# Attention and FFN on one core: the last 1024 queries in five chunks in place of three, and another rank for finishing attention

## The chip, the cores and the metric
The kernel runs on one core of a Trainium2 chip. The metric is device time in microseconds of one execution; the number shown for a kernel is the median of its runs. The core has five engines that run side by side: TensorE (PE: matmuls, with weight loads shown as PEld), VectorE (DVE), ScalarE (ACT), GpSimd (POOL) and SyncE (SP, which here issues DMAs). They wait for one another by semaphores. Matmuls write to PSUM, eight banks of 128 x 512 fp32; the rest lives in SBUF.

## The reference
One pre-layernorm transformer block in bfloat16: sequence S = 2048, width D = 512, 32 heads of 16, FFN width F = 1792.

```python
h  = x + attention(layernorm(x))        # softmax(q k^T / 4) v per head, then @ wo
h2 = h + (gelu(ln(h) @ w_gate) * (ln(h) @ w_up)) @ w_down
```

## The kernel before
**Work.** Scores are made transposed: a *tile* is 128 keys x 512 score columns of one head group, so that exp of it is at once the stationary-side partner of V. Queries come in chunks, `CHUNKS = (512, 512, 512, 256, 256)` (line 1143). A *unit* is one PSUM bank of attention output: 64 tiles (16 key blocks x 4 row groups g). In a chunk of 512 a unit is one head slot; in a chunk of 256 it holds two slots side by side (`per(c) = 512 // CHUNKS[c]`, line 1290). There are 32 units and 2048 tiles for any choice of chunks. One tile's scores are one matmul (line 1532, 32 rows of the array, row group g); its product with V is one matmul per slot (lines 1694 to 1697, a 32-column group of the array each, four groups at once).

**Exp on two engines.** ScalarE takes two tiles per instruction (line 1585) from PSUM banks 0 to 3. VectorE takes tiles in groups of four from the other banks (`dget`, line 1599): one conversion per tile (line 1658), then a chain of three operations for the group (lines 1671, 1673, 1678) with a quarter of the middle one on GpSimd (line 1675). A tile made so needs two products with V per slot, as its value is the product of two fp16 factors accumulated in PSUM.

**End of a unit** (`ofin`, line 1758): VectorE copies the bank to `OA` (line 1762), SP issues a transpose by DMA (line 1769; PE turns the last unit, line 1774), VectorE takes the reciprocal of the softmax sums (line 1778), GpSimd (VectorE for the last unit) multiplies into `Otok` (line 1784). When all units of a chunk have ended, `Otok` is turned (line 1807), and per block of 128 queries `post` (line 1825) projects with `wo`, adds the residual (1845), makes the layernorm (1849 to 1854) and turns the result into `hnT_c` (1857; the last chunk uses PE, 1835 and 1862).

**FFN of a chunk**, beside the attention of the chunks that follow: gates into PSUM (line 1883, through the helper at line 1324), copied to `GUT` (1912); one Gelu over the chunk in two halves on ScalarE (1925), with a table load ahead of it and one back to exp after it; ups, multiplied in place by VectorE (1939); downs per block of 128 queries (1949), the residual add (1958) and the store (1961). The last chunk, behind the last exp, takes Gelu straight from PSUM (1908). `GUT` has 512 query columns; every chunk starts at column 0, and the gates of a chunk wait until the downs of all earlier ones are done (line 1890). A bank is packed with 512 // CHUNKS[c] blocks of F (line 1870).

**Order.** Nothing is ordered by hand: `Sched` (line 889) simulates the engines at build time with a cost per operation and emits, for each engine, the ready operation of lowest rank; ties are spread by a seeded random number (line 906). The chip then runs each engine's list in that order. Ranks that matter here: VectorE's conversions and FFN evacuations stand at -2.2 (`HELD`, line 1117, used in `_rank`, line 934), the chain of a VectorE group at -2.1 or -4 (line 1574), and `ofin` at -3 until its copy is out and at -1 after it (line 1708). FFN matmuls are raised to -6 while `room()` holds, that is while few exp tiles wait for their product with V (`HLAG`, lines 1118 and 2013). `behind()` (line 1310) lets VectorE hold one tile less in PSUM when the FFN of finished chunks lags. `fill` (line 1991) puts matmuls with a zero operand where PE would idle, until 15 of the 16 query blocks are through their downs. A second, safe path (`max_path`) stands in the program and is entered only if a check of the softmax sums at the end asks for it; it does not run here.

**Space.** `h_c` and `hnT_c` of a chunk lie in the part of `QT` that the chunk's end has freed, or in the block of chunk 0 or 1 (`h_at`, line 1244).

Of the kernel before, what the change touches and what calls it, by code (L numbers as in the profile page):

```python
# [888 lines left out]
class Sched:  # L889
# [5 lines left out]
    def __init__(self, P, banks):  # L895
        self.P = P
        self.t = {n: 0.0 for n in P.ENGINES}
        self.done = {}
        self.streams = []
        self.banks = [(0.0, b) for b in banks]  # L900
        self.now = 0.0
        self.fill = None
        self.debt = (0.0, 0.0)
        self.pipe = 0.0
        self.lent = set()
        self.rng = random.Random(16)
# [298 lines left out]
def fast_path(nc, P, base0, ARENA, pbank, flag, A_x, A_wqkv, A_wo, B_x, B_w_gate, B_w_up, B_w_down, out):  # L1205
# [38 lines left out]
    def h_at(c):  # L1244

        if 128 * first_t[c + 1] % 512 == 0:
            c4 = 128 * first_t[c + 1] // 512 - 1
            return 8192 * c4, [("qT", s_, c4) for s_ in range(NSLOT)]
# [7 lines left out]
    h_over = [k for _, k in h_off]  # L1256
# [51 lines left out]
    PIECES = sum(2 * NFC // (512 // n) + n // 128 for n in CHUNKS[:-1])  # L1308

    def behind():  # L1310
        rest = (len(TILES) - C["qpos"]) / (len(TILES) * (1 - CHUNKS[0] / 2048))
# [211 lines left out]
    def scores(put):  # L1523
        fns, rd = [], []
        for i, b in put:
            u, kt, g = TILES[i]
            c, slots = units[u]
            c4, qs = qpart(c)
            n, j = len(slots), slots[0] // 2
            rhs = QT[32 * g:32 * g + 32, c4, slots[0], qs] if n == 1 else QT[32 * g:32 * g + 32, c4, slots[0]:slots[0] + n, qs]  # L1530
            o = pbank[:, b, :] if n == 1 else pbank[:, b, :].rearrange("p (s q) -> p s q", s=n)
            fns.append(MM(o, KT[32 * g:32 * g + 32, j, 128 * kt:128 * kt + 128], rhs, True, True, (32 * g, 0)))
            rd += [("qT", x, c4) for x in slots] + [("kT", j, kt // 4)]
        return fns, sorted(set(rd))

    def qk():
        nxt, an = 0, 0
# [25 lines left out]
    def qk_ready(u):  # L1563
        c, slots = units[u]
        c4, _ = qpart(c)
        keys = [("qT", x, c4) for x in slots] + [("kT", slots[0] // 2, q) for q in range(NCH)]
        return all(k in P.last_writer and sch.done[P.last_writer[k]] <= sch.now for k in keys)

    def close_group():
# [188 lines left out]
    def ofin(u):  # L1758
# [66 lines left out]
    def post(c, qt):  # L1825
# [4 lines left out]
        if c < NC - 1:  # L1830
            yield Wait(lambda: C["ot"] >= first_t[c] + qt + 1)
        else:
            b = yield Acquire(reads=rd, gate=lambda: C["oproj"] >= first_t[c])
            pt = pbank[:, b, :].bitcast(BF16)
            yield Op("pe", 4 * TTR, cols=512, fns=[lambda e, hc=hc: e.transpose(out=pt[:, 128 * hc:128 * hc + 128], in_=Otok[:, cp, qt, 128 * hc:128 * hc + 128], identity=ident[:])
                                 for hc in range(4)], reads=rd, writes=[("pb", b)])
# [37 lines left out]
    gbase = [0]  # L1874
    for c_ in range(NC):
        gbase.append(gbase[-1] + NFC // pack(c_))

    def product(c, k, b, w, rd):
        nq = CHUNKS[c]
        for j in range(pack(c)):  # L1880
            fc = k * pack(c) + j
            for hf in range(2):
                yield Op("pe", 2 * tmm(nq), cols=2 * nq, fns=[MM(pbank[:, b, j * nq:j * nq + nq], w[:, dc, 128 * fc:128 * fc + 128], hnT_c[c][:, :, dc, :], dc == 0, dc == 3)
                                                              for dc in (2 * hf, 2 * hf + 1)], reads=rd, writes=[("pb", b)])

    def gates(c):
        nb = CHUNKS[c] // 128
        rd = ["wg"] + [("hnT", c, q) for q in range(nb)]
        for k in range(NFC // pack(c)):
            b = yield Acquire(reads=rd, gate=lambda: C.get(("hnT", c), 0) == nb and C["down"] >= first_t[c])  # L1890
            yield from product(c, k, b, wg_sb, rd)
            sch.add(gate_evac(c, k, b), base_dl(c) + 29)

    def tmm(n):
        return max(0.09, TMM * n / 512)

    def dE():
        return P.retire([("x", 0, 0), ("x", 0, 1)] + [("x", c) for c in range(1, NCH)] + [("xn", i) for i in range(8)])

    def gslots(c, k):  # L1900
        n = pack(c)
        return GUT[:, n * k:n * k + n, 0:CHUNKS[c]], [("GUT", n * k + j) for j in range(n)]

    def gate_evac(c, k, b):
        o_ap, keys = gslots(c, k)
        i_ap = pbank[:, b, :].rearrange("p (f q) -> p f q", f=pack(c))
        if c == NC - 1:
            yield Op("act", 0.47, lambda e: e.activation(out=o_ap, in_=i_ap, func=ACT.Gelu_apprx_tanh), reads=[("pb", b)], writes=keys)
            sch.release(b)
            C[("gelu", c, k)] = 1  # L1910
            return
        yield Op("dve", 0.6, lambda e: e.tensor_copy(out=o_ap, in_=i_ap), reads=[("pb", b)], writes=keys, extra=dE)  # L1912
        sch.release(b)
        C[("gate", c)] = C.get(("gate", c), 0) + 1
        C["pieces"] += 1
        if C[("gate", c)] == NFC // pack(c):
            sch.add(gelu(c), -5)

    def gelu(c):
        nq = CHUNKS[c]  # L1920
        for hf in range(GSPLIT):
            f0, f1 = NFC * hf // GSPLIT, NFC * (hf + 1) // GSPLIT
            ap = GUT[:, f0:f1, 0:nq]
            keys = [("GUT", f) for f in range(f0, f1)]
            yield Op("act", 0.05 + 0.000833 * nq * (f1 - f0) + TTAB * (hf == 0) + TTAB * (hf == GSPLIT - 1), lambda e, ap=ap: e.activation(out=ap, in_=ap, func=ACT.Gelu_apprx_tanh), reads=keys, writes=keys)
            for k in range(f0 // pack(c), f1 // pack(c)):
                C[("gelu", c, k)] = 1

    def ups(c):
        rd = ["wu"] + [("hnT", c, q) for q in range(CHUNKS[c] // 128)]  # L1930
        for k in range(NFC // pack(c)):
            b = yield Acquire(reads=rd, gate=lambda: ("gelu", c, k) in C)
            yield from product(c, k, b, wu_sb, rd)
            sch.add(up_evac(c, k, b), base_dl(c) + 29)

    def up_evac(c, k, b):
        o_ap, keys = gslots(c, k)
        u_ap = pbank[:, b, :].rearrange("p (f q) -> p f q", f=pack(c))
        yield Op("dve", 0.6, lambda e: e.tensor_tensor(out=o_ap, in0=u_ap, in1=o_ap, op=ALU.mult), reads=[("pb", b)] + keys, writes=keys)  # L1939
        sch.release(b)  # L1940
        C["gut"] += 1
        C["pieces"] += 1

    def downs(c):
        for qt in range(CHUNKS[c] // 128):
            b = yield Acquire(reads=["wd"], gate=lambda: C["gut"] >= gbase[c + 1])
            for f0 in range(0, NFC, 3):
                fcs = list(range(f0, min(NFC, f0 + 3)))
                yield Op("pe", TMM * len(fcs), cols=512 * len(fcs), fns=[MM(pbank[:, b, :], GUT[:, fc, 128 * qt:128 * qt + 128], wd_sb[:, fc, :], fc == 0, fc == NFC - 1)
                                                                         for fc in fcs], reads=["wd"] + [("GUT", fc) for fc in fcs], writes=[("pb", b)])  # L1950
            C["down"] += 1
            C["pieces"] += 1
            sch.add(down_evac(c, qt, b), base_dl(c) + 29)

# [118 lines left out]
```

## Time and profile before
| | |
|---|---|
| median of 9 runs | 820.14 us (819.09 to 820.67) |
| the profiled execution: its own time, its span | 820.55 us, 818.5 us |
| busy over the span: ACT, PE, DVE, POOL | 93%, 94%, 91%, 30% |
| exps on ScalarE / on VectorE | 778 x 2 tiles / 492 tiles |
| fill matmuls (line 1989) | 120 |
| Gelus of chunks 0, 1, 2, 3 begin | 348.3, 526.7, 676.6, 779.6 us |
| last exp ends | 778.3 us |
| last output add begins | 812.9 us |

All times in the profile are from one execution. Times of a group are the sum of its instructions' durations; instructions of an engine overlap a little (an exp shows 1.09 us, and the next starts about 0.92 us after it), so that the distance from start to start is the price of one. TensorE's granted clock is 1.00 nearly throughout (0.90 after 800 us).

### The profile page before, as it was taken

How to read it: one execution, taken by the hardware profiler on the slowest of the kernel's cores; microseconds unless marked ns; L12 is line 12 of the kernel's file. 1: busy time of each engine (PE TensorE's matmuls, PEld its weight loads, DVE VectorE, ACT ScalarE, POOL GpSimd, SP SyncE). 2: the span in 40 equal slices, each digit the busy share in tenths (PEclk: the TensorE clock that was granted, in tenths of full speed). 3: DMA queues.
4: the chain of work that ended last, by engine and by line, in shares of the span. 5: the costliest groups of instructions: out<-in, count | busy, mean ns of one | idle time of the engine just before them, and what ended most of it. 6: DMA issues, size and time to landing. Idle time of an engine off the chain costs nothing. (4 is left out here: it accounts for less than half of the span.)

```text
span 818.5 us, 16590 instructions
## 1 busy us (share of the span) xinstructions
PE 772.4 (94%) x6438; PEld 239.7 (29%) x6500; DVE 744.7 (91%) x1217; ACT 764.1 (93%) x813; POOL 244.5 (30%) x292
## 2 busy tenths in 40 slices
PE   9899999989899999999989899999999998999997
PEld 4222222222222222232222222222233332333464
DVE  7669999899999999999999899999999998998762
ACT  2899999999999999999999999999999999999931
POOL 5703445632332532112222421212223221132200
PEclk9999999999999999999999999999999999999999
DMA  6200000620000210000000210000021000021000
GB/s 206 52 8 2 7 8 7 245 52 8 7 1 1 60 33 1 8 20 14 22 8 1 58 27 8 7 8 20 20 66 21 20 8 8 2 40 40 8 14 18
DMA packets 48776, 23.84 MB, mean 29 GB/s; under 512 B 38192, under 2 KB 47664, under 8 KB 48688
## 3 DMA queue, kind: packets, MB, share of 16 engines
q1 hardware_dynamic: 48688, 22.69, 10.3%
q8 instruction: 53, 0.87, 0.5%
q14 instruction: 35, 0.29, 0.1%
HBM read 11.80 MB, written 2.10 MB: 17 GB/s over the span
## 5 line engine op out<-in xcount | busy, mean ns | idle before, releaser
L1331 ACT ACTIVATE PT<-pbank 128x1024 bf16<-128x1024 f32 x778 | 722.9, 1092 | 13.4 <-PE pbank L1325 11.0
L1325 PE MATMUL pbank<-QT,KT 32*128 32x512 bf16 x2048 | 346.2, 384 | 24.4 <-ACT PT L1331 18.6
L1658 DVE TENSOR_SCALAR dXE<-pbank 128x512 uint16<-128x512 f32 x492 | 323.4, 685 | 11.2 <-PE pbank L1325 9.8
L1675 POOL TENSOR_TENSOR dXE<-dXE 128x512 f16<-128x512 f16 x123 | 154.2, 1253 | 455.2 <-DVE dXE L1673 455.2
L1325 PEld LDWEIGHTS pbank<-QT,KT 32*128 32x128 bf16 x2048 | 86.3, 91 | 326.3 <-ACT PT L1331 245.7
L1325 PE MATMUL pbank<-PT,VA 128*32 128x512 bf16 (+1 forms) x1948 | 129.0, 342 | 1.2 <-DVE h_c L1845 0.7
L1673 DVE TENSOR_TENSOR dXE<-dXE 128x1536 f16<-128x1536 f16 x123 | 118.0, 959 | 1.0
L1678 DVE TENSOR_SCALAR dXE<-dXE 128x2048 uint16<-128x2048 uint16 x123 | 86.5, 704 | 8.7 <-POOL dXE L1675 7.7
L1671 DVE TENSOR_SCALAR dXE<-dXE 128x2048 uint16<-128x2048 uint16 x123 | 89.0, 723 | 0.2
L1325 PE MATMUL pbank<-dXE,VA 128*32 128x512 f16 (+1 forms) x1224 | 75.7, 342 | 3.2 <-DVE dXE L1678 3.0
L1324 PE MATMUL pbank<-hnT_c,wg_sb 128*128 128x512 bf16 (+1 forms) x280 | 67.2, 340 | 0.0
L1324 PE MATMUL pbank<-hnT_c,wu_sb 128*128 128x512 bf16 (+1 forms) x280 | 60.3, 346 | 2.5 <-DVE GUT L1939 2.2
L1324 PE MATMUL pbank<-wd_sb,GUT 128*128 128x512 bf16 x205 | 55.1, 381 | 2.7 <-issue 2.5
L1325 PEld LDWEIGHTS pbank<-PT,VA 128*32 128x32 bf16 x1948 | 36.1, 95 | 62.8 <-issue 59.7
L1939 DVE TENSOR_TENSOR GUT<-pbank,GUT 128x512 bf16<-128x512 f32 x56 | 37.3, 683 | 10.6 <-PE pbank L1324 9.8
L1989 PE MATMUL pbank<-ones_bf,zero_bf 128*128 128x512 bf16 x120 | 42.7, 387 | 1.3 <-issue 1.3
L1324 PE MATMUL pbank<-xnT,wqkv_sb 128*128 128x512 bf16 x128 | 37.3, 383 | 0.8 <-DMA xnT<-xn_sb 0.8
L1912 DVE CAST GUT<-pbank 128x512 bf16<-128x512 f32 x49 | 33.4, 684 | 4.0 <-PE pbank L1324 4.0
L1478 POOL TENSOR_SCALAR QT<-QT,qmask 128x512 bf16<-128x512 bf16 x30 | 25.4, 851 | 24.7 <-DVE QT L1475 23.7
L1325 PEld LDWEIGHTS pbank<-dXE,VA 128*32 128x32 bf16 x1224 | 22.1, 95 | 33.5 <-issue 15.7
L1324 PEld LDWEIGHTS pbank<-hnT_c,wu_sb 128*128 128x128 bf16 x280 | 23.8, 99 | 26.2 <-issue 11.9
L1784 POOL TENSOR_TENSOR Otok<-OAT,LINV 128x256 bf16<-128x256 bf16 (+1 forms) x38 | 24.0, 639 | 12.8 <-DVE LINV L1778 11.9
(87 smaller groups left out, 334.4 us busy)
## 6 DMA issues: line engine op xcount, KB each, us to landing
xres<-in_A_x_dram SPq DMA_DIRECT2D x16, 128.0 KB, 2.1
out_dram<-out_sb SPq DMA_DIRECT2D x16, 128.0 KB, 1.7
wg_sb<-in_B_w_gate_dram SPq DMA_DIRECT2D x1, 1792.0 KB, 7.7
wu_sb<-in_B_w_up_dram SPq DMA_DIRECT2D x1, 1792.0 KB, 11.6
wd_sb<-in_B_w_down_dram SPq DMA_DIRECT2D x1, 1792.0 KB, 15.9
x_sb<-in_A_x_dram SPq DMA_DIRECT2D x3, 512.0 KB, 7.9
wqkv_sb<-in_A_wqkv_dram SPq DMA_DIRECT2D x1, 896.0 KB, 7.1
x_sb<-in_A_x_dram SPq DMA_DIRECT2D x2, 256.0 KB, 2.9
```

The source lines that it names most:

```text
L1324: return lambda e: e.matmul(o, l, r, start=start, stop=stop)
L1325: return lambda e: e.matmul(o, l, r, start=start, stop=stop, tile_position=tile)
L1331: return lambda e: e.activation(out=o, in_=i, func=func, **kw)
L1478: yield Op("pool", 0.85, lambda e, par=par: e.tensor_scalar(out=QT[:, c, 2 * j + par, :], in0=raw, scalar1=qmask[:, par:par + 1], scalar2= ...
L1658: yield Op("dve", 0.603, lambda e: e.tensor_scalar(out=dXE[G["k"] % NX][:, 0, j, :], in0=pbank[:, b, :], scalar1=XMIN + 1024.0 * CENTER, s ...
L1671: yield Op("dve", 0.07 + 0.133 * n, lambda e: e.tensor_scalar(out=W, in0=X, scalar1=0x3ff, scalar2=0xb800, op0=ALU.bitwise_and, op1=ALU.bi ...
L1673: yield Op("dve", 0.066 + 0.267 * nd, lambda e: e.tensor_tensor(out=W[:, 0:nd, :].bitcast(F16), in0=W[:, 0:nd, :].bitcast(F16), in1=X[:, 0 ...
L1675: yield Op("pool", TPOOL, lambda e, j=j: e.tensor_tensor(out=W[:, j, :].bitcast(F16), in0=W[:, j, :].bitcast(F16), in1=X[:, j, :].bitcast( ...
L1678: yield Op("dve", 0.07 + 0.133 * (h1 - h0), lambda e, h0=h0, h1=h1: e.tensor_scalar(out=X[:, h0:h1, :], in0=X[:, h0:h1, :], scalar1=0x7c00 ...
L1912: yield Op("dve", 0.6, lambda e: e.tensor_copy(out=o_ap, in_=i_ap), reads=[("pb", b)], writes=keys, extra=dE)
L1939: yield Op("dve", 0.6, lambda e: e.tensor_tensor(out=o_ap, in0=u_ap, in1=o_ap, op=ALU.mult), reads=[("pb", b)] + keys, writes=keys)
L1989: return Op("pe", TMM, lambda e: e.matmul(pbank[:, b, :], zero_bf[:], ones_bf[:], start=False, stop=False, skip_group_check=True), reads=[ ...
```

## The change
The three last chunks of 512, 256 and 256 queries become 256, 256, 256, 128 and 128. Chunks are given column ranges in `GUT`, so that chunks smaller than 512 can lie side by side and a chunk's gates wait only for chunks whose columns it takes. A unit of a 128-chunk holds four slots of 128 queries: scores of a tile take two matmuls of 256 columns (slots 0-1 and 2-3 have different keys), its products with V four of 128. The end of a unit ranks at -2.3 after its copy, in place of -1. `HLAG` is 6 in place of 8, and the seed is another.

```diff
-        self.rng = random.Random(16)
+        self.rng = random.Random(21)
...
-HLAG = 8
+HLAG = 6
...
-CHUNKS = (512, 512, 512, 256, 256)
+CHUNKS = (512, 512, 256, 256, 256, 128, 128)
...
-        c0 = h_spare.pop(0)
-        return 8192 * c0, [(k, c0, q) for k in ("h", "hnT") for q in range(4)]
+        if h_spare:
+            c0 = h_spare.pop(0)
+            return 8192 * c0, [(k, c0, q) for k in ("h", "hnT") for q in range(4)], first_t[c0 + 1]
+        c4 = 128 * first_t[c] // 512 - 1
+        assert CHUNKS[c] == 128 and CHUNKS[c - 2] == 256
+        return 8192 * c4 + 2048, [("qT", s_, c4) for s_ in range(NSLOT)], 0
...
-            fns.append(MM(o, KT[32 * g:32 * g + 32, j, 128 * kt:128 * kt + 128], rhs, True, True, (32 * g, 0)))
+            for jj in range(max(1, n // 2)):
+                oo, rr = (o, rhs) if n < 4 else (o[:, 2 * jj:2 * jj + 2, :], rhs[:, 2 * jj:2 * jj + 2, :])
+                fns.append((jj, MM(oo, KT[32 * g:32 * g + 32, j + jj, 128 * kt:128 * kt + 128], rr, True, True, (32 * g, 0))))
...
-            sch.add(ofin(u), -1.0).dyn = lambda: -3 if C["oa"] <= u else -1.0
+            sch.add(ofin(u), -1.0).dyn = lambda: -3 if C["oa"] <= u else -2.3
...
-        if otok_n[c] == NSLOT // per(c) - 2:
+        if otok_n[c] == max(1, NSLOT // per(c) - 2):
             sch.add(xres_loads(c), 60)
...
             sch.release(b)
+        yield Wait(lambda: C["down"] >= h_off[c][2])
         b2 = yield Acquire(reads=[("OH", qt), "wo"])
...
-    def pack(c):
-        return 512 // CHUNKS[c]
+    def packs(c):
+        n = 512 // CHUNKS[c]
+        return [(f, min(n, NFC - f)) for f in range(0, NFC, n)]
...
+        o_ = g_at[-1] + CHUNKS[c_ - 1] if c_ else 0
+        g_at.append(o_ if o_ + CHUNKS[c_] <= 512 else 0)
...
+    def gut_free(c):
+        return all(C.get(("down", d), 0) == CHUNKS[d] // 128 for d in range(c) if g_at[d] < g_at[c] + CHUNKS[c] and g_at[c] < g_at[d] + CHUNKS[d])
...
-            b = yield Acquire(reads=rd, gate=lambda: C.get(("hnT", c), 0) == nb and C["down"] >= first_t[c])
+            b = yield Acquire(reads=rd, gate=lambda: C.get(("hnT", c), 0) == nb and gut_free(c))
...
-        return max(0.09, TMM * n / 512)
+        return max(0.056, TMM * n / 512)
...
-        for hf in range(GSPLIT):
-            f0, f1 = NFC * hf // GSPLIT, NFC * (hf + 1) // GSPLIT
-            ap = GUT[:, f0:f1, 0:nq]
+        parts = [(0, NFC // 2), (NFC // 2, NFC)] if nq > 128 else [(0, NFC)]
+        for i, (f0, f1) in enumerate(parts):
+            ap = GUT[:, f0:f1, g_at[c]:g_at[c] + nq]
...
-            b = yield Acquire(reads=["wd"], gate=lambda: C["gut"] >= gbase[c + 1])
+            b = yield Acquire(reads=["wd"], gate=lambda: C.get(("gut", c), 0) == len(packs(c)))
```
By the new rule the chunks' first columns in `GUT` are 0, 0, 0, 256, 0, 256 and 384. The planner's costs of an evacuation and of a Gelu now follow its width (0.07 + 0.001042 us per column on VectorE, 0.05 + 0.00083 on ScalarE), and a 128-column matmul is planned at 0.056 us.

More of the change, by code (lines that the diff above doesn't have):

```diff
@@ L1247, in h_at @@
             c4 = 128 * first_t[c + 1] // 512 - 1
-            return 8192 * c4, [("qT", s_, c4) for s_ in range(NSLOT)]
-        c0 = h_spare.pop(0)
-        return 8192 * c0, [(k, c0, q) for k in ("h", "hnT") for q in range(4)]
+            return 8192 * c4, [("qT", s_, c4) for s_ in range(NSLOT)], 0
+        if h_spare:
[4 more added lines that the diff above has]
+        return 8192 * c4 + 2048, [("qT", s_, c4) for s_ in range(NSLOT)], 0
     h_spare = [0, 1]
@@ L1255, in fast_path @@
     h_off = [h_at(c) for c in range(NC)]
-    h_over = [k for _, k in h_off]
+    h_over = [o[1] for o in h_off]
     h_c = [at("h_c%d" % c, [128, CHUNKS[c] // 128, D], BF16, h_off[c][0]) for c in range(NC)]
@@ L1307, in fast_path @@
     otok_n = {}
-    PIECES = sum(2 * NFC // (512 // n) + n // 128 for n in CHUNKS[:-1])
+    PIECES = sum(2 * -(-NFC // (512 // n)) + n // 128 for n in CHUNKS[:-1])
     def behind():
@@ L1531, in scores @@
             o = pbank[:, b, :] if n == 1 else pbank[:, b, :].rearrange("p (s q) -> p s q", s=n)
-            fns.append(MM(o, KT[32 * g:32 * g + 32, j, 128 * kt:128 * kt + 128], rhs, True, True, (32 * g, 0)))
-            rd += [("qT", x, c4) for x in slots] + [("kT", j, kt // 4)]
-        return fns, sorted(set(rd))
+            for jj in range(max(1, n // 2)):
+                oo, rr = (o, rhs) if n < 4 else (o[:, 2 * jj:2 * jj + 2, :], rhs[:, 2 * jj:2 * jj + 2, :])
+                fns.append((jj, MM(oo, KT[32 * g:32 * g + 32, j + jj, 128 * kt:128 * kt + 128], rr, True, True, (32 * g, 0))))
+            rd += [("qT", x, c4) for x in slots] + [("kT", x // 2, kt // 4) for x in slots]
+        return [f for _, f in sorted(fns, key=lambda a: a[0])], sorted(set(rd))
     def qk():
@@ L1565, in qk_ready @@
         c4, _ = qpart(c)
-        keys = [("qT", x, c4) for x in slots] + [("kT", slots[0] // 2, q) for q in range(NCH)]
+        keys = [("qT", x, c4) for x in slots] + [("kT", x // 2, q) for x in slots for q in range(NCH)]
         return all(k in P.last_writer and sch.done[P.last_writer[k]] <= sch.now for k in keys)
@@ L1867, in post, with gkeys, product @@
         C[("hnT", c)] = C.get(("hnT", c), 0) + 1
-    def pack(c):
-        return 512 // CHUNKS[c]
-    gbase = [0]
+    def packs(c):
+        n = 512 // CHUNKS[c]
+        return [(f, min(n, NFC - f)) for f in range(0, NFC, n)]
+    g_at = []
     for c_ in range(NC):
-        gbase.append(gbase[-1] + NFC // pack(c_))
-    def product(c, k, b, w, rd):
+        o_ = g_at[-1] + CHUNKS[c_ - 1] if c_ else 0
+        g_at.append(o_ if o_ + CHUNKS[c_] <= 512 else 0)
+    def gkeys(c, f):
+        return [("GUT", f, q) for q in range(g_at[c] // 128, (g_at[c] + CHUNKS[c]) // 128)]
+    def gut_free(c):
+        return all(C.get(("down", d), 0) == CHUNKS[d] // 128 for d in range(c) if g_at[d] < g_at[c] + CHUNKS[c] and g_at[c] < g_at[d] + CHUNKS[d])
+    def product(c, f0, n, b, w, rd):
         nq = CHUNKS[c]
-        for j in range(pack(c)):
-            fc = k * pack(c) + j
+        for j in range(n):
+            fc = f0 + j
             for hf in range(2):
@@ L1888, in gates @@
         rd = ["wg"] + [("hnT", c, q) for q in range(nb)]
-        for k in range(NFC // pack(c)):
-            b = yield Acquire(reads=rd, gate=lambda: C.get(("hnT", c), 0) == nb and C["down"] >= first_t[c])
-            yield from product(c, k, b, wg_sb, rd)
+        for k, (f0, n) in enumerate(packs(c)):
+            b = yield Acquire(reads=rd, gate=lambda: C.get(("hnT", c), 0) == nb and gut_free(c))
+            yield from product(c, f0, n, b, wg_sb, rd)
             sch.add(gate_evac(c, k, b), base_dl(c) + 29)
     def tmm(n):
-        return max(0.09, TMM * n / 512)
+        return max(0.056, TMM * n / 512)
     def dE():
@@ L1900, in gslots, with bank_of @@
     def gslots(c, k):
-        n = pack(c)
-        return GUT[:, n * k:n * k + n, 0:CHUNKS[c]], [("GUT", n * k + j) for j in range(n)]
+        f0, n = packs(c)[k]
+        return GUT[:, f0:f0 + n, g_at[c]:g_at[c] + CHUNKS[c]], [x for f in range(f0, f0 + n) for x in gkeys(c, f)], n
+    def bank_of(c, b, n):
+        return pbank[:, b, 0:n * CHUNKS[c]].rearrange("p (f q) -> p f q", f=n)
     def gate_evac(c, k, b):
-        o_ap, keys = gslots(c, k)
-        i_ap = pbank[:, b, :].rearrange("p (f q) -> p f q", f=pack(c))
+        o_ap, keys, n = gslots(c, k)
+        i_ap = bank_of(c, b, n)
         if c == NC - 1:
-            yield Op("act", 0.47, lambda e: e.activation(out=o_ap, in_=i_ap, func=ACT.Gelu_apprx_tanh), reads=[("pb", b)], writes=keys)
+            yield Op("act", 0.05 + 0.00083 * n * CHUNKS[c], lambda e: e.activation(out=o_ap, in_=i_ap, func=ACT.Gelu_apprx_tanh), reads=[("pb", b)], writes=keys)
             sch.release(b)
@@ L1911, in gate_evac @@
             return
-        yield Op("dve", 0.6, lambda e: e.tensor_copy(out=o_ap, in_=i_ap), reads=[("pb", b)], writes=keys, extra=dE)
+        yield Op("dve", 0.07 + 0.001042 * n * CHUNKS[c], lambda e: e.tensor_copy(out=o_ap, in_=i_ap), reads=[("pb", b)], writes=keys, extra=dE)
         sch.release(b)
@@ L1915, in gate_evac @@
         C["pieces"] += 1
-        if C[("gate", c)] == NFC // pack(c):
+        if C[("gate", c)] == len(packs(c)):
             sch.add(gelu(c), -5)
@@ L1920, in gelu @@
         nq = CHUNKS[c]
-        for hf in range(GSPLIT):
-            f0, f1 = NFC * hf // GSPLIT, NFC * (hf + 1) // GSPLIT
-            ap = GUT[:, f0:f1, 0:nq]
[L1924 to L1927, printed above, removed]
+        parts = [(0, NFC // 2), (NFC // 2, NFC)] if nq > 128 else [(0, NFC)]
+        for i, (f0, f1) in enumerate(parts):
+            ap = GUT[:, f0:f1, g_at[c]:g_at[c] + nq]
+            keys = [x for f in range(f0, f1) for x in gkeys(c, f)]
+            yield Op("act", 0.05 + 0.000833 * nq * (f1 - f0) + TTAB * (i == 0) + TTAB * (i == len(parts) - 1), lambda e, ap=ap: e.activation(out=ap, in_=ap, func=ACT.Gelu_apprx_tanh), reads=keys, writes=keys)
+            for k, (f, n) in enumerate(packs(c)):
+                if f + n <= f1:
+                    C[("gelu", c, k)] = 1
     def ups(c):
         rd = ["wu"] + [("hnT", c, q) for q in range(CHUNKS[c] // 128)]
-        for k in range(NFC // pack(c)):
+        for k, (f0, n) in enumerate(packs(c)):
             b = yield Acquire(reads=rd, gate=lambda: ("gelu", c, k) in C)
-            yield from product(c, k, b, wu_sb, rd)
+            yield from product(c, f0, n, b, wu_sb, rd)
             sch.add(up_evac(c, k, b), base_dl(c) + 29)
     def up_evac(c, k, b):
-        o_ap, keys = gslots(c, k)
-        u_ap = pbank[:, b, :].rearrange("p (f q) -> p f q", f=pack(c))
-        yield Op("dve", 0.6, lambda e: e.tensor_tensor(out=o_ap, in0=u_ap, in1=o_ap, op=ALU.mult), reads=[("pb", b)] + keys, writes=keys)
+        o_ap, keys, n = gslots(c, k)
+        u_ap = bank_of(c, b, n)
+        yield Op("dve", 0.07 + 0.001042 * n * CHUNKS[c], lambda e: e.tensor_tensor(out=o_ap, in0=u_ap, in1=o_ap, op=ALU.mult), reads=[("pb", b)] + keys, writes=keys)
         sch.release(b)
-        C["gut"] += 1
+        C[("gut", c)] = C.get(("gut", c), 0) + 1
         C["pieces"] += 1
@@ L1945, in downs @@
         for qt in range(CHUNKS[c] // 128):
-            b = yield Acquire(reads=["wd"], gate=lambda: C["gut"] >= gbase[c + 1])
+            b = yield Acquire(reads=["wd"], gate=lambda: C.get(("gut", c), 0) == len(packs(c)))
             for f0 in range(0, NFC, 3):
                 fcs = list(range(f0, min(NFC, f0 + 3)))
-                yield Op("pe", TMM * len(fcs), cols=512 * len(fcs), fns=[MM(pbank[:, b, :], GUT[:, fc, 128 * qt:128 * qt + 128], wd_sb[:, fc, :], fc == 0, fc == NFC - 1)
-                                                                         for fc in fcs], reads=["wd"] + [("GUT", fc) for fc in fcs], writes=[("pb", b)])
+                q0 = g_at[c] + 128 * qt
+                yield Op("pe", TMM * len(fcs), cols=512 * len(fcs), fns=[MM(pbank[:, b, :], GUT[:, fc, q0:q0 + 128], wd_sb[:, fc, :], fc == 0, fc == NFC - 1)
+                                                                         for fc in fcs], reads=["wd"] + [("GUT", fc, q0 // 128) for fc in fcs], writes=[("pb", b)])
             C["down"] += 1
+            C[("down", c)] = C.get(("down", c), 0) + 1
             C["pieces"] += 1
```

## Prediction
> **What bounds the kernel now.** I read the page's busy times and costliest groups first, then the tile counts of exp by stage, then the timeline around one Gelu, around one late unit, and of the last 40 us.
>
> The page:
> ```profile
> PE 772.4 (94%) x6438; PEld 239.7 (29%) x6500; DVE 744.7 (91%) x1217; ACT 764.1 (93%) x813; POOL 244.5 (30%) x292
> ...
> L1331 ACT ACTIVATE PT<-pbank 128x1024 bf16<-128x1024 f32 x778 | 722.9, 1092 | 13.4 <-PE pbank L1325 11.0
> ...
> L1658 DVE TENSOR_SCALAR dXE<-pbank 128x512 uint16<-128x512 f32 x492 | 323.4, 685 | 11.2 <-PE pbank L1325 9.8
> ```
> ScalarE makes 778 x 2 of the 2048 score tiles, VectorE the other 492. ScalarE idles 13.4 us ahead of its exps: while attention runs, the time is tiles over the joint rate of the two, and whatever else either does costs tiles.
>
> Busy time by stage, of the exps (L1331, two tiles each; the table load after a Gelu has this line too) and then of VectorE's first step (L1658, one tile each); columns: window, its length, busy us (count), granted clock, DMA share, GB/s:
> ```profile
> 200.00:250.00 50.00, 50.00 (x56) 1.00 0.02 4
> 350.00:400.00 50.00, 44.77 (x48) 1.00 0.07 17
> 650.00:700.00 50.00, 41.72 (x46) 0.97 0.03 7
> ```
> ```profile
> 200.00:250.00 50.00, 25.59 (x41) 1.00 0.02 4
> 350.00:400.00 50.00, 21.59 (x33) 1.00 0.07 17
> 650.00:700.00 50.00, 18.69 (x28) 0.97 0.03 7
> ```
> Without FFN work, 112 + 41 = 153 tiles in 50 us; over 150 to 300 us it is 456, or 3.04 per us. In chunk 0's FFN it is 94 + 33 = 127, in chunk 2's 90 + 28 = 118. Summed against 3.04 per us, FFN takes 48 tiles from 250 to 400 us (chunk 0), 62 from 450 to 600 (chunk 1), 67 from 600 to 778 (chunk 2, and chunk 3 up to its gates).
>
> One Gelu, ScalarE's timeline (start, length):
> ```profile
> 343.04 3.92 ACT L1331 ACTIVATE PT<-pbank 128x1024 bf16<-128x1024 f32 x4
> 346.98 1.28 ACT L1925 ACT_TABLE_LOAD   x1
> 348.27 6.27 ACT L1925 ACTIVATE GUT<-GUT 128x3584 bf16<-128x3584 bf16 x2
> 354.56 1.28 ACT L1331 ACT_TABLE_LOAD   x1
> 355.85 2.86 ACT L1331 ACTIVATE PT<-pbank 128x1024 bf16<-128x1024 f32 x3
> ```
> Exp ends at 346.96 and starts at 355.85. With the 0.17 us by which exps otherwise overlap, an interlude costs 9.06 us, 6.27 of it Gelu and 2.8 fixed.
>
> The last 40 us, timeline of PE; 40.2 us run from the last exp's end (778.3) to the end of the span (818.5):
> ```profile
> 781.09 0.61 PE L1835 MATMUL pbank<-ident,Otok 128*128 128x128 bf16 x8
> ...
> 797.05 1.04 PE L1324 MATMUL pbank<-hnT_c,wu_sb 128*128 128x256 bf16 x8
> 797.92 1.04 PE L1324 MATMUL pbank<-hnT_c,wg_sb 128*128 128x256 bf16 x8
> ...
> 806.86 5.99 PE L1324 MATMUL pbank<-wd_sb,GUT 128*128 128x512 bf16 x27
> ```
> PE sets it, nearly gapless: chunk 3's ups and downs, then all of chunk 4.
>
> **Tail, the first gain.** Afterwards only chunk 6, 128 queries, lies whole behind the last exp. Its chain, by the same steps for one tile: last exp 778.3, unit copied 779.0, turned 779.8, h from 783.5, LN2's result 786.3, hnT 787.2 to 787.6: 9.3 us, and 0.2 more for two more slots of Otok. Meanwhile PE has what is left of chunk 5, at most 3 us of ups and 3 of downs. Then 112 gate and up matmuls of 128 columns. No such product is in the trace; the bounds are 56 ns, from eight 128-column transposes with eight weight loads in 0.61 us ((0.61 - 0.22)/7), and 109 ns, the 256-column row (0.87 us for 8): 6.3 or 12.2 us. I take 56, whose width is the same, and 0.4 us for seams as now (12.65 us against 112 x 0.109). Downs: 14 x 0.217 = 3.0; output add 0.7; from its end to the span's end 4.95 as now (813.57 to 818.5). Sum: 9.5 + 6.7 + 3.0 + 0.7 + 4.95 = 24.8 us in place of 40.2: **15.4 us saved**.
>
> **What moves under attention, the price.** Now 1536 queries' FFN are complete before the last exp, and 256 queries have LN2 and gates. Afterwards 1792 are complete and 128 have LN2 and gates.
> - ScalarE: now 3 interludes, 27.2 us. After: 2 of 9.06 and 3 of 256 queries (2.8 + 3.28, from the two 1.69 us Gelus at 779.6) = 36.4. That is +9.2 us, if chunk 5's Gelu falls at the end, as chunk 3's does now (778.3).
> - VectorE: a 512-chunk has 28 evacuations, 4 outputs, 4 residual adds and 4 statistics at 0.6, 4 aggregates at 0.1 and 4 normalisations at 0.33 us start to start, 25.7 us. So +12.85 for 256 queries, less 4.3 for 128 queries' LN2 and gates: +8.5 us. The remainder of two blocks in a 128-chunk's four banks costs one instruction more and is nothing beside that.
> - In tiles: ScalarE makes one in 0.457 us, VectorE one in 1.12 (0.60 convert and 2.07/4 chain). (9.2/0.457 + 8.5/1.12)/3.04 = 9.1 us. The same sum gives 43 tiles for chunk 0 where 48 were lost, so I raise it by 48/43: **10.2 us**.
>
> The skill's page "ScalarE: Activation LUTs", section "What ACT_TABLE_LOAD costs", puts a switch at about 2.66 us with its drain, 5.3 an interlude; the interlude above has 2.8 for both switches. By the page the two further interludes would cost some 5 us more of ScalarE (an estimate), 3.6 in time; the row decides.
>
> **Narrow attention matmuls.** Chunks 5 and 6 issue four 128-column PV products per tile, and two score products of 256. PV runs in four column groups at once; these are two widths in PE's timeline:
> ```profile
> 422.62 0.62 PE L1325 MATMUL pbank<-PT,VA 128*32 128x512 bf16 x8
> ```
> ```profile
> 767.65 0.62 PE L1325 MATMUL pbank<-dXE,VA 128*32 128x256 f16 x16
> ```
> Sixteen at half width took what eight took: one step of four per 109 ns, so chunk 2's move to 256 costs nothing. For 128, 256 tiles x 1.24 (VectorE's count double, 24% of tiles) x 4 = 1270 products, 318 steps: between 56 ns (the transposes) and 109 ns a step, 17.8 or 34.7 us. I take 56, as the transposes' width is this one, so no extra; the other end is +17 us in the last 95 us, where PE is 97% busy and nothing hides it. Two 256-column score products at 109 ns equal one of 512.
>
> The skill's "TensorE: Matmul & The Clock Gate", section "Wait — 56ns, not 53.3ns?", gives a floor of about 25 ns from start to start however narrow a matmul is. If it held across the four column groups, 1270 x 25 = 32 us, +14, an estimate that speaks against the change; the 256-wide row, at 27 ns per matmul, does not tell.
>
> **Finishing ahead of exp tiles, the second gain.** One unit's end (VectorE's timeline):
> ```profile
> 688.15 0.68 DVE L1762 CAST OA<-pbank 128x512 bf16<-128x512 f32 x1
> ...
> 723.02 0.69 DVE L1658 TENSOR_SCALAR dXE<-pbank 128x512 uint16<-128x512 f32 x1
> 723.63 0.24 DVE L1778 RECIPROCAL LINV<-OAT 128x16 f32<-128x16 bf16 x1
> ```
> The transpose by DMA of about 2.5 us went out at 688.9; the reciprocal, ranked -1 behind conversions at -2.2, came 32 us later, and chunk 3's LN2 only at 738. Chunks 0 and 1 end in the same way: unit 7 is copied at 220.5 and in Otok at 270.0, unit 15 at 397.9 and 450.1. At -2.3 it goes ahead; the work is the same, and what is late is a conversion, by 0.25 us, 32 times: covered by the second tile that VectorE may hold in PSUM, and 8 us of one bank's time if it is not. FFN then starts 30 to 50 us sooner, where PE still issues fill matmuls, and the planner's "behind", which lets VectorE hold one tile in PSUM and not two, holds less often. Bounds: nothing, or all that chunks 1 and 2 lost beyond chunk 0's measure (62 - 48 and 67 - 57 tiles), 8 us. I take 3.
>
> **The rest.** Side-by-side columns of GUT let chunk 3's gates pass chunk 2's downs; PE is busy there either way. The new wait of a chunk's projection for an earlier chunk's downs holds only that stream: for chunk 2 these end by 412 us, for chunk 4 by 603, both before its attention does. SP issues two transposes by DMA more (chunk 6 has one tile on PE, not two). HLAG and the seed reorder ties: a gain is bounded by ScalarE's waits for PE, 11 us; for a loss I use the 5 us by which chunk 1's FFN cost more than chunk 0's (14 tiles). I take nothing.
>
> **Sum.** Last exp at 778.3 + 10.2 - 3 = 785.5; + 24.8 = 810.3 of span. The profiled run took 820.55 with a span of 818.5: +2.05. The median is 0.4 lower: **812.0 us**.
>
> **Rivals.**
> - All 8 us come back: 807. With a part of the 11 us of ScalarE's waits, down to 801. For it: chunk 0 against chunk 1. Against: the last stage ends its VectorE tiles early in any case.
> - The price eats the gain. Nothing comes back, the price is that of all chunks (177 tiles lost for 136 computed, so 11.9 us), and chunk 5's Gelu and ups land before the last exp (+4.5 ScalarE, +2.7 VectorE, 4 us): 794.2 + 24.8 + 1.65 = 820.7, no change.
> - Idle PE in the 9.5 us chain: fills stop once 15 tiles are down, and if chunk 5 is done by then the clock falls (now it is granted 0.90 after 800 us). Gates and ups at 109 ns, +6: 818.
> - Slower: PE becomes the bound in chunks 5 and 6 because 128-wide PV steps don't shrink to 56 ns. At 109 ns: 829; it decides from about 85 ns (+8 us and past 820).
>
> **Numbers.** Forecast with its idle-PE variant 0.55, all back 0.13, price eats gain 0.12, PE bound 0.20. Measurement tells 0.2%, 1.6 us. Faster 0.70, same 0.10, slower 0.20. Range 801 to 824: it leaves out the upper part of the PE case and a little below.
>
> **What would show it.** In the profile afterwards: last exp near 785 and 25 us behind it; 128-column FFN matmuls 56 ns apart; 32 PV products of 128 in about 0.6 us; Gelu interludes of 6 us; reciprocals within 5 us of their copy; about as many VectorE tiles as now. A last exp past 794 or a tail over 32 us would make it wrong.

## The result and the profile after
The changed kernel takes 830.55 us (median of 10 runs, 825.0 to 842.3) against 820.14 us: ratio 1.0105, interval 1.0093 to 1.0118. It is 1% slower, where 812 (1% faster) was forecast. The runs spread because TensorE's granted clock differs from run to run, and the ratios, the line through runs below and the table of seeds leave out those in which it was lowest. The profiled execution took 830.51 us with a span of 828.8; the lines below are its own (line numbers are some 4 to 21 higher than before).

The page of the changed kernel: busy times, the granted clock in 40 slices, and the two exp groups.
```profile
PE 776.5 (94%) x8186; PEld 275.2 (33%) x8262; DVE 760.7 (92%) x1231; ACT 770.2 (93%) x813; POOL 249.0 (30%) x307
...
PEclk9999999996799999999999999999999999999999
...
L1335 ACT ACTIVATE PT<-pbank 128x1024 bf16<-128x1024 f32 x776 | 724.7, 1063 | 24.7 <-PE pbank L1329 21.5
...
L1664 DVE TENSOR_SCALAR dXE<-pbank 128x512 uint16<-128x512 f32 x496 | 326.1, 683 | 17.8 <-PE pbank L1329 16.1
```
The split of exp between the engines is as it was (776 x 2 and 496 tiles). New are 10.5 us more of ScalarE's waiting for PE (21.5 for 11.0), and two slices near 200 us in which the clock reads 6 and 7.

ScalarE's timeline where attention ends:
```profile
794.14 5.61 ACT L1335 ACTIVATE PT<-pbank 128x1024 bf16<-128x1024 f32 x6
799.76 1.28 ACT L1985 ACT_TABLE_LOAD   x1
```
The last exp ends at 799.7, not 785.5; the tail behind it is 29.0 us (forecast 24.8, before 40.2). So 21.4 us are lost under attention and 11.2 won in the tail.

The stretch of the clock dip, first the changed kernel and then the one before; columns are busy us and count of PE, PEld, DVE, ACT and POOL, then granted clock, DMA share, GB/s:
```profile
150.00:191.00 41.00, 36.86 (x303) 9.99 (x307) 40.16 (x60) 40.90 (x46) 17.01 (x14) 1.00 0.42 148
191.00:218.00 27.00, 25.72 (x138) 4.81 (x137) 19.14 (x30) 20.05 (x21) 4.84 (x4) 0.50 0.03 6
```
```profile
150.00:191.00 41.00, 36.02 (x310) 9.69 (x305) 39.65 (x64) 40.97 (x46) 16.18 (x16) 1.00 0.44 148
191.00:218.00 27.00, 24.75 (x203) 7.05 (x204) 26.01 (x42) 27.00 (x30) 9.45 (x8) 1.00 0.03 6
```
At half clock ScalarE made 21 exps where it made 30, VectorE's conversions (counted by their line) are 19 where they were 23: 61 tiles for 83. The 22 missing are **7.2 us** at 3.04 per us. This is attention alone; no FFN and no small chunk is in it. The runs of the changed kernel say the same: at a mean clock of 0.980 they take 830.5 us, at 0.985 829.9, at 0.991 826.3; a line through nine runs falls 4.6 us per 0.01, and carried on to the 0.9975 about which the kernel before runs it gives 823. The kernel before has a low clock too, but rarely: of its 74 runs on record one has 0.982, and takes 829.3 us.

### The profile page after: what moved, and what is told of

The parts are those of the page before. It is cut to its first block, busy times and chain, and to the rows that moved or that the text cites. A ratio compares the mean times of both kernels' runs of the same rounds, so it can differ in the third digit from the quotient of the medians.

```text
span 828.8 us, 20124 instructions
## 1 busy us (share of the span) xinstructions
PE 776.5 (94%) x8186; PEld 275.2 (33%) x8262; DVE 760.7 (92%) x1231; ACT 770.2 (93%) x813; POOL 249.0 (30%) x307
## 3 DMA queue, kind: packets, MB, share of 16 engines
q1 hardware_dynamic: 49776, 22.95, 10.5%
## 4 chain that ended last, share of the span: by engine, by line
PE 53%; ACT 18%; DVE 17%; issue 8%; POOL 2%; DMA 2%; ACTq 0%; DVEq 0%; POOLq 0%
PE pbank L1329 34%; ACT PT L1335 17%; PE pbank L1328 16%; DVE dXE L1664 6%; DVE dXE L1679 2%; DVE dXE L1684 2%; DVE dXE L1677 2%; PE pbank L2010 2%; PE pbank L2006 1%; POOL dXE L1681 1%; DMA OAT<-OA 1%; ACT GUT L1943 1%; DVE GUT L1930 1%; DMA hnT_c<-OnT 1%; DVE stats L1856 0%
## 5 line engine op out<-in xcount | busy, mean ns | idle before, releaser
L1335 ACT ACTIVATE PT<-pbank 128x1024 bf16<-128x1024 f32 x776 | 724.7, 1063 | 24.7 <-PE pbank L1329 21.5
L1329 PE MATMUL pbank<-QT,KT 32*128 32x512 bf16 (+1 forms) x2304 | 350.5, 365 | 28.0 <-ACT PT L1335 20.2
L1329 PE MATMUL pbank<-PT,VA 128*32 128x256 bf16 (+2 forms) x2700 | 132.9, 297 | 0.5 <-DVE VA L1502 0.5
L1329 PE MATMUL pbank<-dXE,VA 128*32 128x256 f16 (+2 forms) x1768 | 78.2, 293 | 4.1 <-DVE dXE L1684 2.7
L1328 PE MATMUL pbank<-hnT_c,wg_sb 128*128 128x256 bf16 (+2 forms) x392 | 69.5, 291 | 0.8 <-DMA hnT_c<-OnT 0.7
L1329 PEld LDWEIGHTS pbank<-PT,VA 128*32 128x32 bf16 x2700 | 48.5, 97 | 64.1 <-issue 60.6
L1328 PE MATMUL pbank<-hnT_c,wu_sb 128*128 128x256 bf16 (+2 forms) x392 | 59.3, 289 | 2.6 <-DVE GUT L1958 1.7
L1790 POOL TENSOR_TENSOR Otok<-OAT,LINV 128x128 bf16<-128x128 bf16 (+2 forms) x52 | 24.5, 487 | 122.3 <-DVE LINV L1784 122.3
L1329 PEld LDWEIGHTS pbank<-dXE,VA 128*32 128x32 bf16 x1768 | 32.3, 97 | 34.5 <-issue 18.6
L1958 DVE TENSOR_TENSOR GUT<-pbank,GUT 128x512 bf16<-128x512 f32 (+1 forms) x57 | 36.9, 674 | 3.0 <-PE pbank L1328 2.7
L1930 DVE CAST GUT<-pbank 128x512 bf16<-128x512 f32 (+1 forms) x53 | 35.7, 678 | 0.4 <-PE pbank L1328 0.2
```

Of the source, the lines that this page charges most:

```text
L1328: return lambda e: e.matmul(o, l, r, start=start, stop=stop)
L1329: return lambda e: e.matmul(o, l, r, start=start, stop=stop, tile_position=tile)
L1335: return lambda e: e.activation(out=o, in_=i, func=func, **kw)
L1930: yield Op("dve", 0.07 + 0.001042 * n * CHUNKS[c], lambda e: e.tensor_copy(out=o_ap, in_=i_ap), reads=[("pb", b)], writes=keys, extra=dE)
L1958: yield Op("dve", 0.07 + 0.001042 * n * CHUNKS[c], lambda e: e.tensor_tensor(out=o_ap, in0=u_ap, in1=o_ap, op=ALU.mult), reads=[("pb", b)] ...
```

## Experiments
Theory 1: the clock dip is the loss, and the chunks gain. Rival (theory 2): the chunks themselves cost.

**The three order edits without the chunks**
```diff
-        self.rng = random.Random(16)
+        self.rng = random.Random(21)
-HLAG = 8
+HLAG = 6
-    sch.add(ofin(u), -1.0).dyn = lambda: -3 if C["oa"] <= u else -1.0
+    sch.add(ofin(u), -1.0).dyn = lambda: -3 if C["oa"] <= u else -2.3
```


> The kernel before with the rank of finishing attention at -2.3, HLAG 6 and seed 21; the chunks stay 512, 512, 512, 256, 256. Theory 1 (the clock): the changed order leaves PE too little work in some 3.4 us around 190 us, the granted clock falls to 0.5 there for 27 us, and the change loses some 12 us in it, whatever the chunks: the dip shows here too, between 150 and 250 us, and the time is 820 + 12 less what the earlier end of attention is worth (some 3 to 8), so 824 to 830. Theory 2 (the chunks): the small chunks cost the time: no dip that matters here, 812 to 820.


831.2 us (ratio 1.0125, 1.0099 to 1.0151), last exp 786.8, tail 41.5. No long dip in the profiled execution: two of 3.4 us. The loss is there without the chunks, against theory 2; without the dip at 190 us too, against theory 1 as worded.

**The chunks without the order edits** (the changed kernel with `random.Random(16)`, `HLAG = 8` and rank -1.0)


> The changed kernel with the rank -1.0, HLAG 8 and seed 16 of before; only the chunks are new. Theory 1: the order until 250 us is nearly that of before, so the clock stays up there; the last exp ends near 788 and the time is 814 to 820. Theory 2: 826 or more with the clock at 0.99 or higher.


829.3 us (1.0116, 1.0102 to 1.0129), clock 0.996, last exp 784.4, tail 40.5. The price under attention is 6.1 us, but the tail does not get shorter: with finishing at -1, the two units of chunk 5 have their reciprocals 11.9 and 31.4 us after their copies, and chunk 5's residual add waits until 792. The time and the clock are those of theory 2, so that neither theory fits both runs. Against the run of rank and chunks below, which differs in the rank alone (824.4 us, tail 29.4), the small chunks need the rank.

**More fill matmuls** (`RATE = 1200` in place of 950), in the changed kernel and, as control, in the one before


> The changed kernel with RATE 1200 in place of 950: the planner keeps PE at 1200 columns per us by fill matmuls with zeros, so more of them in the attention-only stage. Theory 1: no half clock between 150 and 250 us, mean granted clock 0.99 or more, last exp near 788, time 815 to 820 and the runs within 0.5% of one another. Theory 2: the same clock gain at most, but the time stays above 826.

> Control: the kernel before with RATE 1200. Its clock is full already, so both theories expect nothing but the price of more fills: 820 to 822. If it gets faster than 817, more fills are worth something beside the clock, and the run of the changed kernel with them is no proof for theory 1.


The changed kernel goes to 825.2 us (1.0063, 1.0051 to 1.0075), between the two theories. The dip at 190 is gone and there are 194 fills in place of 102, but the last exp is at 801.3, no earlier than the 799.7 with the dip; the tail is 25.0. Part of that is a trade: here chunk 5's Gelu, with its two table loads, comes before the last exp and not behind it. The control missed by far: 849.9 us, with 241 fills for 120, three dips around 300 us and 37 us of ScalarE's waiting for PE. More fills are no clean test of the clock, and no remedy.

**One order edit at a time**, each on the kernel before


> The kernel before with nothing changed but the rank of finishing attention (-2.3). Theory A (the rank costs by itself: VectorE's conversions come later, FFN earlier, and the end does not move): reciprocals 4 us behind their copy, last exp near 786 as in the run with all three order edits, time 826 to 830. Theory B (any redraw of the planner's list loses about 1%, as the list of before is a chosen draw): about the same time for this, for HLAG alone and for the seed alone. Theory C (the rank gains, seed or HLAG lose): 815 to 820.

> The kernel before with HLAG 6 and nothing else. Theory A: within 0.3% of before, 818 to 822. Theory B: 825 to 832. Theory C: one of this run and the seed's loses 8 us or more.

> The kernel before with seed 21 and nothing else; the same operations with ties drawn anew. Theory A: within 0.3% of before. Theory B: 825 to 832, with as many tiles per engine as before to within some 10 and the loss spread over the stages. Theory C: one of this run and HLAG's loses 8 us or more.

> The changed kernel with HLAG 8 and seed 16 of before: the chunks and the rank. Theory 1 (the clock dip of the changed kernel comes with its draw): no dip between 150 and 250 us, last exp near 788, the tail 29 as in the changed kernel, so 816 to 821. Theory A: last exp at 784 + 8 = 792 or later and 822 or more. Theory B gives 825 to 832, as any redraw.


The rank alone gives 827.35 us (1.0092, 1.0077 to 1.0106), HLAG alone 824.3 (1.0046, 1.0033 to 1.0059), the seed alone 835.9 (1.0208, 1.0192 to 1.0223). All three lose, the seed most, and a seed leaves the work as it is, but for the fills (154 for 120) and four tiles that change from ScalarE to VectorE. So HLAG and the seed are not free, against theory A, and the three losses are not alike, against theory B as worded here; a loss of 8 us or more by the seed is what theory C named. Rank and chunks together give 824.4 (1.0072, 1.0046 to 1.0097), above theory 1's 816 to 821: the chunks are 3 us better than the rank alone. ScalarE's last exp in the run of the rank, and in that of rank and chunks:
```profile
775.25 6.73 ACT L1331 ACTIVATE PT<-pbank 128x1024 bf16<-128x1024 f32 x7
782.00 1.28 ACT L1964 ACT_TABLE_LOAD   x1
```
```profile
785.67 7.87 ACT L1335 ACTIVATE PT<-pbank 128x1024 bf16<-128x1024 f32 x8
793.56 1.28 ACT L1985 ACT_TABLE_LOAD   x1
```
With spans of 823.5 and 823.0, the chunks cost 11.5 us under attention and save 12.1 behind it. That is one profiled execution of each, and the chunks give the planner another list as well.

In the run of the seed alone, ScalarE's waits between 285 and 330 us:
```profile
ACT PT L1331 <- PE pbank L1325: 18.7, 2, 18.3
```
One wait of 18.3 us. Ahead of it units 6 and 7 have had their copies out at 196.9 and 216, and get their reciprocals together at 305.3, 108 and 89 us late; the control with 241 fills shows the same (112 us late, one wait of 19.8 us). My reading, not tested, is that starved unit ends stop the PV banks, then PE, then ScalarE; the clock is down to 0.76 between 290 and 325 us as well, and the runs do not part the two. At rank -2.3 the worst delay in any run was 17 us and ScalarE's longest wait for PE 4.7 us.

**Seeds**, for both kernels (`random.Random(n)` is the only edit)


> The changed kernel with seed 16. Theory B (the seed is a draw that moves any of these kernels by some 10 us, and the kernel before has a chosen one): at one seed the change itself is worth between -6 and +6 us; here against before (also 16) that means 814 to 826, and no dip of the clock as at 21 need show. Theory A (the rank and the chunks cost by themselves): 826 to 832 at every seed.

> The kernel before with seed 17. Theory B: a fresh draw of the same kernel lands above before, 824 to 836. Theory A: 818 to 823, seed 21 having been a bad draw.

> The changed kernel with seed 17, to be set against before at 17. Theory B: at or below it (at 21 the pair is 835.9 and 830.6). Theory A: 5 us or more above it.

> The kernel before with seed 18: as for 17. Theory B 824 to 836, theory A 818 to 823.

> The changed kernel with seed 18; the kernel before took 836.7 at this seed. Theory B (before has a chosen draw; at any other seed the change gains 5 to 14 us): 822 to 831. Theory A (chunks and rank cost by themselves): 838 or more.

> The kernel before with seed 19. Theory B: 826 to 839 like 17, 18 and 21. Theory A: 818 to 823, and three bad draws were chance.

> The changed kernel with seed 19; the kernel before took 833.5 at this seed. Theory B as it stands after the other pairs: 822 to 834, some 5 us below. Theory A: 836 or more.

| seed | the kernel before, us | the changed kernel, us |
|---|---|---|
| 16 (before) | 820.1 | 823.6 |
| 17 | 832.1 | 824.4 |
| 18 | 836.7 | 837.7 |
| 19 | 833.5 | 827.0 |
| 21 (changed) | 835.9 | 830.5 |

The kernel before loses 12 to 17 us at each of four other seeds: of the five, 16 is its exception. At those four the changed kernel is at -7.7, +1.0, -6.5 and -5.4 us, on the mean 829.9 against 834.5; from the spread of the four differences, their mean of -4.6 is known to some 6 us (an estimate), so a gain is suggested and not shown. At seed 16 the change costs 3.5 us (1.0051, 1.0035 to 1.0068). The weakest pair is that at 17, where the runs of the kernel before lie between 828.4 and 845.2. The pair at 18 fits neither theory (822 to 831, or 838 and more). The draws of the changed kernel differ among themselves by 14 us. At 18 it has the clock at 0.977, with dips of 20.5 us at 190 and 10.2 at 412.

**Chunk 5's late layernorm.** VectorE's timeline in the changed kernel: end of chunk 5's attention, residual add, aggregate, normalisation, and the first of its gates:
```profile
759.46 0.25 DVE L1784 RECIPROCAL LINV<-OAT 128x16 f32<-128x16 bf16 x1 [0.89 <-DMA OAT<-OA]
...
768.62 0.69 DVE L1852 TENSOR_TENSOR h_c<-pbank,xres 128x512 bf16<-128x512 f32 x1
...
779.91 0.17 DVE L1857 BATCH_NORM_AGGREGATE mv<-stats 128x2 f32<-128x6 f32 x1
...
787.67 0.41 DVE L1861 TENSOR_SCALAR OnT<-h_c,mv,rstd 128x512 bf16<-128x512 bf16 x1
...
797.13 0.69 DVE L1930 CAST GUT<-pbank 128x512 bf16<-128x512 f32 x1
```
Nineteen us from residual add to normalised rows, where the last chunk needs 3. So I raised that rank for chunks 4 and 5:
```diff
-                sch.add(post(c, qt), -2.5 if c == NC - 1 else base_dl(c) + qt * 2)
+                sch.add(post(c, qt), -2.5 if c >= NC - 3 else base_dl(c) + qt * 2)
```


> The changed kernel with seed 16 and the rank of the projection and layernorm 2 of chunks 4 and 5 at -2.5, ahead of VectorE's exp tiles. Theory D (chunk 5's late layernorm makes the tail 29 and not 25 us): residual add of chunk 5 to its normalised rows in 5 us instead of 19, its gates before the last exp, tail 24 to 26, last exp 2 us later for the work moved, time 3 us below the 823.6 of seed 16: 819 to 822. Rival: the gates wait for PE's turn anyway; tail 28 to 30 and 823 to 826.

> The same at seed 21. The list is that of the changed kernel until chunk 4's attention ends, so the clock dip at 190 us stays and with it the spread of times; theory D: tail 24 to 26 and about 828 where the changed kernel took 830.5; rival: 830 or more.


At seed 16: residual add to normalised rows in 2.7 us, tail 26.7 us instead of 29.2; but the last exp is at 804.2 instead of 791.5, and the time 828.7 us (1.0099, 1.0082 to 1.0116) instead of 823.6. At seed 21: tail 26.7, last exp 804.9, 834.0 us (1.0194, 1.0129 to 1.0259). The tail moved as theory D said, though not quite to its 24 to 26; the time went the other way, past the rival's too. ScalarE's timeline of the run at seed 16 shows one reason:
```profile
791.56 1.28 ACT L1943 ACT_TABLE_LOAD   x1
792.85 1.70 ACT L1943 ACTIVATE GUT<-GUT 128x1792 bf16<-128x1792 bf16 x1
794.57 1.28 ACT L1335 ACT_TABLE_LOAD   x1
795.86 8.36 ACT L1335 ACTIVATE PT<-pbank 128x1024 bf16<-128x1024 f32 x9
```
With its gates earlier, chunk 5's Gelu falls before the last exp and costs exps 4.3 us there (791.54 to 795.86; the same 4.3 at seed 21), more than the 2.5 by which the tail got shorter.

The other reason is the clock: 17.1 us of this execution are at half clock from 192.5 us on, which that of seed 16 without the raised rank has not. Up to 713 us ScalarE and VectorE run the same instructions in the same order in both, so that this pair shows what a dip costs, apart from any redraw. Three units' copies on VectorE, first without the raised rank, then with it:
```profile
174.00 0.68 DVE L1768 CAST OA<-pbank 128x512 bf16<-128x512 f32 x1
198.79 0.68 DVE L1768 CAST OA<-pbank 128x512 bf16<-128x512 f32 x1
219.16 0.68 DVE L1768 CAST OA<-pbank 128x512 bf16<-128x512 f32 x1
```
```profile
174.97 0.68 DVE L1768 CAST OA<-pbank 128x512 bf16<-128x512 f32 x1
203.41 0.69 DVE L1768 CAST OA<-pbank 128x512 bf16<-128x512 f32 x1 [0.26 <-PE pbank L1329]
224.65 0.68 DVE L1768 CAST OA<-pbank 128x512 bf16<-128x512 f32 x1
```
The distance grows from 1.0 to 5.5 us and does not come back (6.0 at 713 us): 17.1 us at half clock cost 4.5, and 27.3 us of it, as in the changed kernel, would cost 7.2 at that rate (an estimate). No version with these chunks beat the kernel before.

**Only the third 512 split** (chunks 512, 512 and four of 256, rank -2.3, HLAG 8, seed 16)


> Chunks of 512, 512 and four of 256, with the rank -2.3, HLAG 8 and seed 16: set between the run of the rank alone (last exp 782.0, tail 41.5) and that of rank and chunks (793.5 and 29.4). If the two chunks of 128 pay: tail 38 to 42, last exp 785 to 788 for two more table-load pairs beside Gelu less the work that stays behind, 826 to 829, 2 us or more above the 824.4 of rank and chunks. If they don't: 822 or less.


828.4 us (1.0104, 1.0087 to 1.0121), last exp 791.4, tail 35.5. Against the rank alone (782.0 and 41.5) splitting the third 512 costs 9.4 us and saves 6.0; splitting the last 256 then costs 2.1 and saves 6.1. At these draws the two chunks of 128 pay, with 4.0 us, and the third 512 in halves does not. The time is as expected if the small chunks pay; last exp and tail are not (785 to 788 and 38 to 42 were expected), and 4 us is less than draws of one kernel differ by.

## Why the prediction was wrong
In the order of its steps, with the last exp's forecast of 778.3 + 10.2 - 3 + 0 against 778.3 + 11.5 + 3.7 + 6.2 (chunks, rank, HLAG and seed, from the runs above). Two terms failed, the 3 us for finishing ahead and the nothing for HLAG and the seed. Each edit also redraws the planner's list, so the terms measured here hold for these draws. The last exp at 799.7 is past the 794 that the prediction named as a sign of being wrong; the other signs came out as said, but for a tail of 29.0 us in place of 25 and one reciprocal 11.2 us behind its copy.

- **Tail: right in kind, 12.1 of 15.4 us.** The narrow products went at the width's price. PE's timeline of the changed kernel, up and gate matmuls of the last chunk:
```profile
815.18 1.06 PE L1328 MATMUL pbank<-hnT_c,wg_sb 128*128 128x128 bf16 x16
816.07 1.06 PE L1328 MATMUL pbank<-hnT_c,wu_sb 128*128 128x128 bf16 x16
```
16 in 0.89 us, 56 ns each. What was missed is chunk 5: I left it "at most 3 us of ups and 3 of downs"; in fact 30 of its 56 gate matmuls came after the last exp as well, and everything behind them. Gates and ups of chunk 6 began 10.3 us behind the last exp (9.5) and with chunk 5's downs among them took 9.8 us (6.7); the end took 5.2 (4.95). The forecast also had a tail of 24.8 with chunk 5's Gelu in it and not in the price. In the runs with small chunks at rank -2.3 it is one or the other: a tail of 25.0 to 26.7 us where that Gelu comes before the last exp, at 4.3 us there (seed 17, more fills, both runs of the late layernorm), and 28.5 to 29.4 where it comes behind (the other five).
- **Price under attention: near, 11.5 for 10.2.** The rate of 3.04 tiles per us counts exps at a window's edge in both windows; by their starts it is 444 tiles in 150 us, 2.96, and the same sum then gives 9.6. The 4.3 us for LN2 and gates of 128 queries come to 3.7 by the prediction's own prices, which adds 0.2. A Gelu interlude of 256 queries, ScalarE:
```profile
654.39 6.52 ACT L1335 ACTIVATE PT<-pbank 128x1024 bf16<-128x1024 f32 x7
660.93 1.28 ACT L1943 ACT_TABLE_LOAD   x1
662.22 3.29 ACT L1943 ACTIVATE GUT<-GUT 128x1792 bf16<-128x1792 bf16 x2
665.52 1.28 ACT L1335 ACT_TABLE_LOAD   x1
666.82 1.94 ACT L1335 ACTIVATE PT<-pbank 128x1024 bf16<-128x1024 f32 x2
```
From 660.91 to 666.82 and 0.17 for the overlap: 6.08 us, as forecast.
- **Narrow attention matmuls: right.** The rival that gave the slower side, 128-wide PV steps that bind PE in chunks 5 and 6, is false although its time, 829, is near the result:
```profile
776.78 0.63 PE L1329 MATMUL pbank<-dXE,VA 128*32 128x128 f16 x32
...
777.67 0.63 PE L1329 MATMUL pbank<-PT,VA 128*32 128x128 bf16 x32
```
32 products in what 16 took before. The floor of 25 ns for each, which the prediction took from its page as a case against the change, would have made 0.8 us; it does not hold across the four column groups.
- **Finishing ahead of exp tiles: the step whose mechanism failed.** The edit did what it says: reciprocals come 4.1 us after their copies on the mean, 17.9 before. But "FFN then starts 30 to 50 us sooner" bought nothing at the end. In the run of the rank alone chunks 0 and 1 reach their residual adds at 227 and 414 us for 277 and 461, then FFN stands idle until the next chunk's attention ends; chunk 2 reaches them at 606 in both, as unit 23 was only 7.7 us late before; and chunk 3, 39 us sooner (699 for 738), waits for chunk 2's downs, whose last output is at 766.8 for 751.9: its first gate matmul is at 766.9 for 752.4. I had read the late unit and not the gate behind it (line 1890). Forecast -3 us of last exp; measured +3.7, and +1.3 of tail (by the medians of the runs, +7.2). That nothing was gained is explained so; whether the 5 us lost are the rank's or a redraw's is not told apart.
- **"HLAG and the seed reorder ties": the term taken at nothing.** +6.2 us (830.5 for 824.4; the last exp too), and +6.9 for the seed alone in the changed kernel (830.5 for 823.6). The clock dip with its 7.2 covers either. I had looked for the clock in the tail alone, and had bounded a loss by 5 us where draws of the kernel before differ by 17.

Of the measured +10.4 us, 3.5 are what the change costs at seed 16, and 6.9 came with seed 21. The forecast's -8 lies within what the pairs at the other four seeds leave possible (-4.6 on the mean, known to some 6 us, with one of four against), but they do not show it: rank, chunks and the kernel before's good draw at seed 16 are not told apart. What a dip costs is shown; the way from a draw to its dips and waits is open.

## What to carry to other kernels
When a list is drawn by a seeded planner, the number before a change can be a lucky draw (here by 12 to 17 us against four others): measure the change and its predecessor at several seeds, and give a redraw the spread of those as its bound. Where all engines are full, sooner is no gain by itself: follow an earlier step to the next gate ahead of the end before crediting it. Work moved from a tail under attention cost about what it saved (11.5 for 12.1 us in the one pair here), so book each piece, as chunk 5's Gelu, on one side or the other.

## What the runs showed of the hardware
The clock fell without any long pause of PE. Timeline of PE in the changed kernel, up to the dip:
```profile
188.32 0.39 PE L1329 MATMUL pbank<-QT,KT 32*128 32x512 bf16 x2
189.11 0.39 PE L1329 MATMUL pbank<-QT,KT 32*128 32x512 bf16 x2 [0.40 <-ACT PT L1335]
190.02 0.68 PE L1329 MATMUL pbank<-QT,KT 32*128 32x512 bf16 x3 [0.53 <-ACT PT L1335]
190.64 0.62 PE L1329 MATMUL pbank<-PT,VA 128*32 128x512 bf16 x8
191.19 1.03 PE L1329 MATMUL pbank<-QT,KT 32*128 32x512 bf16 x3
192.15 1.05 PE L1329 MATMUL pbank<-dXE,VA 128*32 128x512 f16 x8
```
Eight products with V take 0.62 us at 190.64, and eight at 192.15 take 1.05. The longest gap in the 20 us ahead is 0.53 us; in the 3.4 us before the fall PE is busy 2.47 us, nearly all of it with 32-row or 32-column matmuls and with no fill among them. It then stayed at half clock for 27 us while PE was busy 25.7 of 27 us. The Trainium skill's page "TensorE: Matmul & The Clock Gate", section "HAM oscillation — how this bites in real kernels", gives as the abstract rule that PE should have no idle gaps over some 3.4 us; here the clock fell with gaps of a sixth of that, so keeping the rule did not keep the clock. Nor do the gaps set the two kernels apart: from 186 to 192 us PE waits 0.9 us in the changed kernel and 1.1 in the one before, 0.5 at the longest in both, and the one before kept its clock. What tipped it is open.
